# Attention with a threshold: each tile's bias from VectorE's product of scores and -c2

## The chip, the cores and the metric

The kernel runs on one core of a Trainium2 chip. The metric is the device time of one execution in microseconds. The kernel before takes 2197.92 us, the median of three runs (2195.69 to 2199.4).

## What is computed

Three blocks follow one another. The first is attention over 4 batches, 8 heads, 576 tokens and a head size of 64, in which each row keeps only the scores within tau (0.02) of its largest; then a gated MLP (512 to 1536 and back) behind an RMS norm; then a mixture of eight experts with weights P from eight Sinkhorn rounds. The part that the change touches:

```python
scores = scale * np.matmul(q, k.transpose(0, 1, 3, 2))
thresh = np.max(scores, axis=-1, keepdims=True) - tau
scores = np.where(scores >= thresh, scores, -1000000000.0)
scores = scores - np.max(scores, axis=-1, keepdims=True)
attn = np.exp(scores)
attn = attn / (np.sum(attn, axis=-1, keepdims=True) + 1e-09)
return np.matmul(attn, v).astype(np.float32)
```

## The kernel before, in words

All matrix products run in fp16 pairs (a high part and a remainder), so inputs are scaled by powers of two: `s_q` and `s_k` are the scales of q and k, `i_q` and `i_k` their inverses, and the score in PSUM is the true one times both scales.

Attention works in tiles of 128 query rows against all 576 keys: 32 tiles per batch of one head each (four chunks `c` of 128 tokens, eight heads) and four tiles of two heads for the remaining 64 tokens, so 36 per batch and 144 in all. `att_tile` does one of them:

- TensorE writes the scores S into PSUM, 128 x 576 in two banks (L282), from q and from the remainder of q. There are two score buffers.
- VectorE takes the maximum of each row, `mx` (L292).
- ScalarE multiplies `mx` by `wt`, which is -c2 (L293): the bias. Then it writes e = exp(c2 * S + bias) as fp32 to SBUF (L296), and adds `bt`, the scaled -tau, to `mx`: the threshold (L297).
- VectorE multiplies e by (S >= threshold) and sums the row in the accumulator (L298). After that the score buffer is free.
- ScalarE casts e to fp16 (L303), GpSimd subtracts for the remainder (L304 and L305), SP's queue transposes both by DMA into eT (L307). e, hl and eT have three buffers each.

`att_values` multiplies eT by v (L330), three tiles later (LAG is 3), issued behind the scores of a later tile. When a chunk's eight heads are through, `end_main` and `finish_x` normalise its rows and transpose them to xnT (L376 to L357). Two chunks make a token tile of the MLP: `mlp_in` (gv, L530, with the gating at L538 to L545) and `mlp_out` (x, L561). The weights of the MLP are prepared meanwhile by `prep_in` and `prep_out` (L432 to L509), and k, v and q of the next batch by `prepare` (L225, L256 and others). The expert block (h, L860; y, L906) comes after it.

The order on each engine is not written out: a planner sorts the instructions of every engine once, by priority, by its own simulated time and by when buffers come free. Attention has the higher priority, MLP work fills in. Once planned, each engine runs its list in order and stops at a wait.

`prep_q_scales` makes the factors of a batch, one column per chunk: `bt` (L207), `c2` (L209) and `wt` (L210), each in a buffer of its own batch. `mx`, the bias and the threshold are three columns of one small tile `nt` with four buffers.

Of the kernel before, what the change touches and what calls it, by code (L numbers as in the profile page):

```python
# [7 lines left out]
F32 = mybir.dt.float32  # L8
# [3 lines left out]
AF = mybir.ActivationFunctionType  # L12
ALU = mybir.AluOpType
AX = mybir.AxisListType
# [5 lines left out]
def kernel(  # L20
# [24 lines left out]
    V, A, G, T = nc.vector, nc.scalar, nc.gpsimd, nc.tensor  # L45
    B, H, S, D = q.shape
# [3 lines left out]
    P = 128  # L50
# [6 lines left out]
    NW = NCH + 1  # L57
# [3 lines left out]
    def small(shape, name, dt=F32, bufs=1):  # L61
        return p0.tile(shape, dt, tag=name, name=name, bufs=bufs)
# [80 lines left out]
    pa = pa_cm.__enter__()  # L143
# [19 lines left out]
    def norm_scale(sq, n, bits, name):  # L163

        return pow2_scale(sq, n, bits, name, 2.0**-60, True)
# [27 lines left out]
    def prep_q_scales(st):  # L193

        b, qr = st["b"], st["raw_q"]
        s_k, i_k = st["k"]
        qm = small([P, NW], "qm", bufs=2)
        for c in range(NW):
            sq = pa.tile([P, H, 2, D], F16, tag="ks", name=f"qq{b}_{c}", bufs=2)
            A.activation(  # L200
                sq[:, :, 0, :].bitcast(BF16), qr[:, :, c, :], AF.Square, accum_out=qm[:, c : c + 1]
            )
        s_q, i_q = norm_scale(qm, NW, 9, f"q{b}")

        wt = small([P, NW], f"wt_{b}")
        bt = small([P, NW], f"bt_{b}")
        V.tensor_scalar(bt, s_q, s_k[:, 0:1], ntau8[:, 0:1], ALU.mult, ALU.mult)  # L207
        c2 = small([P, NW], f"c2_{b}")
        V.tensor_scalar(c2, i_q, i_k[:, 0:1], z8[:, 0:1], ALU.mult, ALU.mult)  # L209
        V.tensor_scalar(wt, i_q, i_k[:, 0:1], nz8[:, 0:1], ALU.mult, ALU.mult)  # L210
        st.update(wt=wt, bt=bt, c2=c2, s_q=s_q)

    def prep_k(st, a):

# [56 lines left out]
    def att_tile(st, c, heads, slot, group):  # L271

        kT = st["kT"]
        qT, qX = st["q", c]
        nm = f"{st['b']}_{c}_{heads[0]}"
        sums = group["sums"]
        sp = psa.tile([P, 2, 512], F32, tag="S", name=f"S{nm}", bufs=2)
        rows = P // len(heads)
        for qq, first in ((qT, True), (qX, False)):
            for i, h in enumerate(heads):  # L280
                for j in range(2):
                    last = T.matmul(  # L282
                        sp[i * rows : (i + 1) * rows, j, 0:HS],
                        lhsT=qq[:, h, 0:rows],
                        rhs=kT[h // H2][:, h % H2, j * HS : (j + 1) * HS],
                        start=first,
                        stop=not first,
                    )
        sv = sp[:, :, 0:HS]
        nt = pa.tile([P, 3], F32, tag="nt", name=f"nt{nm}", bufs=4)  # L290
        mx = nt[:, 2:3]
        V.tensor_reduce(mx, sv, AX.XY, ALU.max)  # L292
        A.activation(nt[:, 0:1], mx, AF.Copy, scale=st["wt"][:, c : c + 1])  # L293
        e = pa.tile([P, S], F32, tag="e", name=f"e{nm}", bufs=3)
        ev = e.rearrange("p (a n) -> p a n", a=2)
        A.activation(ev, sv, AF.Exp, bias=nt[:, 0:1], scale=st["c2"][:, c : c + 1])  # L296
        A.activation(nt[:, 1:2], mx, AF.Identity, bias=st["bt"][:, c : c + 1])  # L297
        V.scalar_tensor_tensor(  # L298
            ev, sv, nt[:, 1:2], ev, ALU.is_ge, ALU.mult, accum_out=sums[:, slot : slot + 1]
        )  # L300

        hl = pa.tile([P, 2 * S], F16, tag="hl", name=f"hl{nm}", bufs=3)
        A.activation(hl[:, 0:S], e, AF.Copy)  # L303
        G.tensor_tensor(hl[:, S + REM :], e[:, 0 : NCH * P], hl[:, 0 : NCH * P], ALU.subtract)  # L304
        G.tensor_tensor(hl[:, S : S + REM], e[:, NCH * P :], hl[:, NCH * P : S], ALU.subtract)  # L305
        eT = pa.tile([P, 2 * S // P, P], F16, tag="eT", name=f"eT{nm}", bufs=3)
        nc.sync.dma_start_transpose(out=eT, in_=hl)  # L307
        waiting.append((st, heads, slot, group, eT))
        if len(waiting) > LAG:

            with tc.issue_after(last.ins):
                att_values(*waiting.pop(0))

    def att_values(st, heads, slot, group, eT):
        if slot == 0:
            group["pv"] = psa.tile([P, H * D], F32, tag="pv", name=f"pv{group['n']}", bufs=1)
        rows = P // len(heads)
        for i, h in enumerate(heads):
            vs, hh = st["vs"][h // H2], h % H2
            o = group["pv"][i * rows : (i + 1) * rows, slot * D : (slot + 1) * D]  # L320
            cols = slice(i * rows, (i + 1) * rows)
            mm = []
            for cc in range(NCH):
                mm.append((eT[:, cc, cols], vs[:, 0, hh, cc, :]))
                mm.append((eT[:, cc, cols], vs[:, 1, hh, cc, :]))
                mm.append((eT[:, NW + cc, cols], vs[:, 0, hh, cc, :]))
            mm.append((eT[:, NCH, cols], vs[:, 0, hh, NCH, :]))
            mm.append((eT[:, NCH, cols], vs[:, 1, hh, NCH, :]))
            for n, (a, r) in enumerate(mm):
                T.matmul(o, lhsT=a, rhs=r, start=n == 0, stop=n == len(mm) - 1)  # L330
        if slot == group["last"]:
            ended.append(group)
# [296 lines left out]
    def prepare(b, o):  # L629

        st = states[b]
        if o < NCH * H and o % H == 1:
            prep_q(st, o // H + 1)
        if b > 0 and o in (LAG - 3, LAG - 1):
            prep_v(st, (o - LAG + 3) // 2)
        if b + 1 == B:
            return
        nx = states[b + 1]
        early = b > 0
        if o == (4 if early else 20):  # L640
            nx["raw_k"] = load_raw("k", k, b + 1)
            nx["raw_v"] = load_raw("v", v, b + 1)
        if o == (10 if early else 23):
            prep_k_scale(nx)
        if o == (12 if early else 24):
            prep_v_scale(nx)
        if o == (18 if early else 26):
            prep_k(nx, 0)
        if o == 25:
            nx["raw_q"] = load_raw("q", q, b + 1)  # L650
        if o == 28:
            prep_q_scales(nx)
        if o == 32:
            prep_q(nx, 0)
        if o == 34:
            prep_k(nx, 1)

    st = states[0]
    for nm, src in (("k", k), ("v", v), ("q", q)):
        st["raw_" + nm] = load_raw(nm, src, 0)  # L660
    prep_k_scale(st)
    prep_q_scales(st)
    prep_q(st, 0)
    prep_k(st, 0)
# [6 lines left out]
    for t in range(len(row) + LAG):  # L671
        before = tc.cur_priority
        with attention_order():
            if t < len(row):
                b, c, heads, n, g = row[t]
                if n == 0:
                    g["sums"] = pa.tile([P, H], F32, tag="sums", name=f"sums{g['n']}", bufs=2)
                att_tile(states[b], c, heads, n, g)
                prepare(b, t % SLOTS)
            else:  # L680
                att_values(*waiting.pop(0))
            done = list(ended)
            ended.clear()
            for g in done:
                (end_main if g["c"] < NCH else end_rem)(g)
        first += tc.cur_priority - before
        for g in done:
            i = g["i"]
            if i == 1:
                for gi in range(NG):  # L690
                    prep_group(gi)
                first = tc.cur_priority
                tT = mlp_in(0)
                prep_out()
                mlp_out(0, tT)
            elif i is not None and i % 2 == 1 and i < len(tiles) - 1:
                mlp_out(i // 2, mlp_in(i // 2))
# [283 lines left out]
```

## Time and profile before

| what | value |
|---|---|
| median of three runs | 2197.92 us |
| profiled execution | 2195.02 us, its span 2193.2 us |
| TensorE (PE) busy | 2032.0 us, 93% |
| VectorE (DVE) busy | 1490.2 us, 68% |
| ScalarE (ACT) busy | 870.9 us, 40% |
| GpSimd (POOL) busy | 471.0 us, 21% |
| mean granted clock of TensorE | 0.98 |
| first and last scores (L282) | 38.9 and 610.6 us |
| first matmul of the MLP (gv, L530) | 156.7 us |

In the rows below times are in microseconds, and ns where that is said. A group's row has the line, the engine, the operation, what it writes and reads by the program's names, shapes, count, then busy time with the mean in ns of one, and idle time of the engine ahead of it. A row of waits has what waited, for whom, the total, how often and the longest. A row of the timeline has its start, its length, the engine and the instruction.

### The profile page before, as it was taken

How to read it: one execution, taken by the hardware profiler on the slowest of the kernel's cores; microseconds unless marked ns; L12 is line 12 of the kernel's file. 1: busy time of each engine (PE TensorE's matmuls, PEld its weight loads, DVE VectorE, ACT ScalarE, POOL GpSimd, SP SyncE). 2: the span in 40 equal slices, each digit the busy share in tenths (PEclk: the TensorE clock that was granted, in tenths of full speed). 3: DMA queues.
4: the chain of work that ended last, by engine and by line, in shares of the span. 5: the costliest groups of instructions: out<-in, count | busy, mean ns of one | idle time of the engine just before them, and what ended most of it. 6: DMA issues, size and time to landing. Idle time of an engine off the chain costs nothing.

```text
span 2193.2 us, 35334 instructions
## 1 busy us (share of the span) xinstructions
PE 2032.0 (93%) x13872; PEld 1194.7 (54%) x13872; DVE 1490.2 (68%) x3026; ACT 870.9 (40%) x1774; POOL 471.0 (21%) x572
## 2 busy tenths in 40 slices
PE   1358789899999999999999999999999999999999
PEld 0236667666876755545555555555555555555554
DVE  6999677777744287865775765766757757666554
ACT  6878778877843243311221221222212212222111
POOL 1347556665743231000000000000000000000000
PEclk9859999999999999999999999999999999999999
DMA  9895879867826051000100100100001001000001
GB/s 267 207 201 100 169 145 174 159 144 115 147 55 142 18 144 40 29 30 1 39 20 20 39 20 20 39 20 20 20 20 39 20 20 39 20 20 1 1 28 60
DMA packets 321879, 154.10 MB, mean 70 GB/s; under 512 B 278960, under 2 KB 292400, under 8 KB 321712
## 3 DMA queue, kind: packets, MB, share of 16 engines
q1 hardware_dynamic: 321120, 151.82, 30.4%
q8 instruction: 108, 1.77, 0.3%
q14 instruction: 59, 0.48, 0.1%
q0 software_dynamic: 64, 0.00, 0.0%
q10 hardware_dynamic: 528, 0.02, 0.0%
HBM read 68.18 MB, written 12.98 MB: 37 GB/s over the span
## 4 chain that ended last, share of the span: by engine, by line
PE 70%; DVE 2%; DMA 1%; SPq 1%; POOL 0%; issue 0%; ACT 0%; DVEq 0%; ACTq 0%
PE y L906 33%; PE h L860 28%; PE gv L530 5%; PE x L561 2%; PE pv L330 1%; DMA w1r<-in_moe_w_dram 1%; SPq L762 0%; PE S L282 0%; DMA x2T<-x2d 0%; DVE w L714 0%; DMA w2r<-in_moe_w_dram 0%; DMA eT<-hl 0%; PE logits L804 0%; DVE w1m L725 0%; POOL xh L601 0%
## 5 line engine op out<-in xcount | busy, mean ns | idle before, releaser
L860 PE MATMUL h<-x2T,w 128*128 128x384 f16 x4032 | 703.8, 326 | 9.9 <-DMA x2T<-x2d 3.9
L860 PEld LDWEIGHTS <-w 128*128 128x128 f16 x4032 | 394.1, 98 | 300.0 <-issue 14.2
L921 DVE SCALAR_TENSOR_TENSOR acc<-y,coef,acc 128x512 f32<-128x512 f32 x270 | 198.1, 746 | 283.0 <-PE y L906 282.9
L730 POOL TENSOR_TENSOR w1s<-w1r 128x512 f32<-128x512 f32 x16 | 20.3, 1271 | 1060.3 <-DMA w1r<-in_moe_w_dram 1006.3
L304 POOL TENSOR_TENSOR hl<-e,hl 128x512 f16<-128x512 f32 x144 | 172.8, 1200 | 228.2 <-ACT hl L303 146.2
L906 PE MATMUL y<-w,hD 128*128 128x512 f16 x864 | 219.9, 379 | 0.0
L906 PE MATMUL y<-w,hA 128*128 128x512 f16 x864 | 210.6, 379 | 0.9 <-DVE acc L921 0.6
L906 PE MATMUL y<-w,hC 128*128 128x512 f16 x864 | 210.0, 379 | 0.2 <-ACT acc L917 0.2
L906 PE MATMUL y<-w,hB 128*128 128x512 f16 x864 | 210.0, 379 | 0.0
L848 ACT ACTIVATE hA<-u 128x384 f16<-128x384 f32 x96 | 50.2, 522 | 341.1 <-DVE u L876 320.9
L848 ACT ACTIVATE hB<-u 128x384 f16<-128x384 f32 x96 | 50.2, 523 | 312.1 <-DVE u L880 311.2
L530 PE MATMUL gv<-xnT,wg 128*128 128x256 f16 x1296 | 167.8, 278 | 4.5 <-DVE u L540 3.0
L530 PE MATMUL gv<-xnT,wv 128*128 128x256 f16 x1296 | 167.5, 275 | 0.0
L330 PE MATMUL pv<-vs,eT 128*128 128x64 f16 (+1 forms) x2240 | 103.1, 201 | 50.3 <-DMA eT<-hl 47.3
L561 PE MATMUL x<-wo,tT 128*128 128x512 f16 x648 | 144.4, 379 | 1.0 <-DVE u L540 0.9
L906 PEld LDWEIGHTS <-hB 128*128 128x128 f16 x864 | 84.5, 98 | 101.9
L530 PEld LDWEIGHTS <-wg 128*128 128x128 f16 x1296 | 126.5, 100 | 24.0 <-issue 4.1
L298 DVE SCALAR_TENSOR_TENSOR e<-S,nt,e 128x576 f32<-128x576 f32 x144 | 116.3, 809 | 32.0 <-ACT e L296 31.5
L906 PEld LDWEIGHTS <-hD 128*128 128x128 f16 x864 | 84.6, 98 | 95.4
L530 PEld LDWEIGHTS <-wv 128*128 128x128 f16 x1296 | 126.4, 99 | 16.0 <-issue 0.2
L906 PEld LDWEIGHTS <-hC 128*128 128x128 f16 x864 | 84.7, 98 | 91.9 <-issue 0.3
L330 PEld LDWEIGHTS <-eT 128*128 128x128 f16 (+1 forms) x2240 | 91.0, 106 | 79.1 <-DMA eT<-hl 62.1
(244 smaller groups left out, 2852.1 us busy)
## 6 DMA issues: line engine op xcount, KB each, us to landing
w1r<-in_moe_w_dram SPq DMA_DIRECT2D x16, 1024.0 KB, 4.9
w2r<-in_moe_w_dram SPq DMA_DIRECT2D x16, 1024.0 KB, 5.3
wgatew<-in_moe_w_gate_dram SPq DMA_DIRECT2D x12, 512.0 KB, 6.0
wo<-in_moe_w_out_dram SPq DMA_DIRECT2D x12, 512.0 KB, 4.2
wvalw<-in_moe_w_val_dram SPq DMA_DIRECT2D x12, 512.0 KB, 4.5
x2d<-xs SPq DMA_DIRECT2D x24, 256.0 KB, 2.5
qX<-qT SPq DMA_DIRECT2D x40, 128.0 KB, 3.5
raw_k<-in_k_dram SPq DMA_DIRECT2D x4, 1024.0 KB, 6.2
```

The lines of the kernel that those rows point to most:

```text
L298: V.scalar_tensor_tensor(ev, sv, nt[:, 1:2], ev, ALU.is_ge, ALU.mult, accum_out=sums[:, slot : slot + 1])
L304: G.tensor_tensor(hl[:, S + REM :], e[:, 0 : NCH * P], hl[:, 0 : NCH * P], ALU.subtract)
L330: T.matmul(o, lhsT=a, rhs=r, start=n == 0, stop=n == len(mm) - 1)
L530: T.matmul(gv[:, a, :], lhsT=w[:, l, kk, f * P : (f + 1) * P], rhs=xt[:, r * KD + kk, :], start=n == 0, stop=n == 3 * KD - 1,)
L561: T.matmul(ps, lhsT=tT[f][:, l, o : o + P], rhs=wo[:, f, r, :], start=n == 0, stop=n == 3 * KF - 1,)
L730: G.tensor_tensor(sm[:, 0], a21, a22, ALU.add)
L848: A.activation(t[:, 0, :], src, AF.Relu)
L860: T.matmul(ps, lhsT=w[:, a, l, kk, f * P : (f + 1) * P], rhs=xb[:, b * 4 + r * 2 + kk, :], start=n == 0, stop=n == 5,)
L906: T.matmul(ps, lhsT=hs[a][f][:, l, jj * P : (jj + 1) * P], rhs=w2[:, r, f, :], start=n == 0, stop=n == 3 * KH - 1,)
L921: V.scalar_tensor_tensor(acc[i], ps, coef[h][:, i : i + 1], acc[i], ALU.mult, ALU.add)
```

## The change

The maximum over the scores is replaced by a product of the scores and `wt` that VectorE writes into e (where the exponential later overwrites it) and whose smallest value in each row goes through the accumulator into the first column of `nt`: since `wt` is negative, that is the bias itself. ScalarE's small multiplication falls away. The threshold is computed from the bias: times `w1`, which is 1 / (-(i_q * i_k) / 8), plus `bt`. `w1` is made per batch by two small VectorE operations. `wt`, `bt`, `c2` and `w1` share two buffers over the batches.

```diff
-        wt = small([P, NW], f"wt_{b}")
-        bt = small([P, NW], f"bt_{b}")
+        wt = small([P, NW], "wt", bufs=2)
+        bt = small([P, NW], "bt", bufs=2)
         V.tensor_scalar(bt, s_q, s_k[:, 0:1], ntau8[:, 0:1], ALU.mult, ALU.mult)
-        c2 = small([P, NW], f"c2_{b}")
+        c2 = small([P, NW], "c2", bufs=2)
         V.tensor_scalar(c2, i_q, i_k[:, 0:1], z8[:, 0:1], ALU.mult, ALU.mult)
         V.tensor_scalar(wt, i_q, i_k[:, 0:1], nz8[:, 0:1], ALU.mult, ALU.mult)
-        st.update(wt=wt, bt=bt, c2=c2, s_q=s_q)
+
+        w1 = small([P, NW], "w1", bufs=2)
+        V.tensor_scalar(w1, i_q, i_k[:, 0:1], -(float(D) ** -0.5), ALU.mult, ALU.mult)
+        V.reciprocal(w1, w1)
+        st.update(w1=w1, wt=wt, bt=bt, c2=c2, s_q=s_q)
...
-        nt = pa.tile([P, 3], F32, tag="nt", name=f"nt{nm}", bufs=4)
-        mx = nt[:, 2:3]
-        V.tensor_reduce(mx, sv, AX.XY, ALU.max)
-        A.activation(nt[:, 0:1], mx, AF.Copy, scale=st["wt"][:, c : c + 1])
+        nt = pa.tile([P, 2], F32, tag="nt", name=f"nt{nm}", bufs=4)
         e = pa.tile([P, S], F32, tag="e", name=f"e{nm}", bufs=3)
         ev = e.rearrange("p (a n) -> p a n", a=2)
+        V.tensor_scalar(
+            ev, sv, st["wt"][:, c : c + 1], None, ALU.mult, ALU.min, accum_out=nt[:, 0:1]
+        )
         A.activation(ev, sv, AF.Exp, bias=nt[:, 0:1], scale=st["c2"][:, c : c + 1])
-        A.activation(nt[:, 1:2], mx, AF.Identity, bias=st["bt"][:, c : c + 1])
+        A.activation(
+            nt[:, 1:2], nt[:, 0:1], AF.Identity, bias=st["bt"][:, c : c + 1],
+            scale=st["w1"][:, c : c + 1],
+        )
```

## Rows read from the trace of the kernel before

**Rows 1.** The page's chain that ended last: share of the span by engine.
```profile
PE 70%; DVE 2%; DMA 1%; SPq 1%; POOL 0%; issue 0%; ACT 0%; DVEq 0%; ACTq 0%
```

**Rows 2.** Busy time by stage: stretch, length, engines (instructions), granted clock, DMA share, GB/s.
```profile
41.00:157.00 116.00, 47.73 (x372) 27.05 (x371) 111.07 (x235) 97.15 (x201) 41.85 (x44) 0.75 0.85 206
157.00:300.00 143.00, 123.12 (x1340) 95.02 (x1339) 114.66 (x271) 112.14 (x263) 89.03 (x112) 0.97 0.73 143
300.00:612.00 312.00, 291.51 (x3222) 219.34 (x3219) 233.09 (x550) 245.04 (x567) 197.46 (x273) 0.98 0.79 145
```

**Rows 3.** Waits of TensorE from 40 to 160 us: total, times, longest.
```profile
PE pv L330 <- DMA eT<-hl: 24.6, 8, 4.7
PE S L282 <- DVE e L298: 19.1, 7, 6.9
```

**Rows 4.** The same from 160 to 620 us.
```profile
PE pv L330 <- DMA eT<-hl: 22.7, 21, 3.8
PE S L282 <- DVE e L298: 5.2, 5, 1.9
```

**Rows 5.** The tile nt: durations in ns, smallest, median, largest.
```profile
L292 DVE TENSOR_REDUCE nt<-S x144: 698/750/759, 41.4 to 611.2; 128x1 f32<-128x576 f32 x144
L293 ACT ACTIVATE nt<-nt,wt x144: 277/286/298, 44.3 to 612.0; 128x1 f32<-128x1 f32 x144
L297 ACT ACTIVATE nt<-nt,bt x144: 277/279/298, 44.5 to 612.2; 128x1 f32<-128x1 f32 x144
L298 DVE SCALAR_TENSOR_TENSOR e<-S,nt,e x144: 758/810/820, 48.4 to 613.2; 128x576 f32<-128x576 f32 x144
```

**Rows 6.** Timeline of VectorE from 130 to 142 us.
```profile
130.71 0.74 DVE L292 TENSOR_REDUCE nt<-S 128x1 f32<-128x576 f32 x1
131.37 0.47 DVE L336 TENSOR_SCALAR rsum<-sums 128x8 f32<-128x8 f32 x1
...
137.50 0.81 DVE L298 SCALAR_TENSOR_TENSOR e<-S,nt,e 128x576 f32<-128x576 f32 x1
138.24 0.08 DVE L298 DVE_READ_ACCUMULATOR e<-S,nt,e 128x1 f32 x1
138.24 0.68 DVE L436 SCALAR_TENSOR_TENSOR wo<-wo,wol 128x512 int32<-128x512 int32 x1
...
140.18 0.75 DVE L292 TENSOR_REDUCE nt<-S 128x1 f32<-128x576 f32 x1
```

**Rows 7.** Timeline of ScalarE from 128 to 148 us (start, length).
```profile
133.65 0.28 ACT L293 ACTIVATE nt<-nt,wt 128x1 f32<-128x1 f32 x1
...
134.95 0.81 ACT L296 ACTIVATE e<-S,nt,c 128x576 f32<-128x576 f32 x1
...
140.97 0.30 ACT L293 ACTIVATE nt<-nt,wt 128x1 f32<-128x1 f32 x1
...
141.35 0.82 ACT L296 ACTIVATE e<-S,nt,c 128x576 f32<-128x576 f32 x1
```

**Rows 8.** Timeline of TensorE: the first matmuls of the MLP.
```profile
156.66 2.74 PE L530 MATMUL gv<-xnT,wg 128*128 128x256 f16 x12 [1.36 <-DMA xnT<-xn]
```

**Rows 9.** Groups by line, shapes apart, of VectorE and of ScalarE.
```profile
L920 DVE TENSOR_SCALAR acc<-acc,coef 128x512 f32<-128x512 f32 x18 | 7.3, 478 | 0.0
L210 DVE TENSOR_SCALAR wt<-q_i,k_i,nz 128x5 f32<-128x5 f32 x4 | 1.2, 300 | 0.0
...
L200 ACT ACTIVATE qq<-raw_q 128x512 bf16<-128x512 f32 x20 | 12.4, 621 | 6.2 <-DMA raw_q<-in_q_dram 6.1
L346 ACT ACTIVATE xn<-x,v_i 128x512 bf16<-128x512 f32 x16 | 11.4, 712 | 3.8 <-DMA xnT<-xn 3.8
```

**Rows 10.** Timeline of VectorE and GpSimd at two of three places.
```profile
248.39 0.75 DVE L292 TENSOR_REDUCE nt<-S 128x1 f32<-128x576 f32 x1
249.11 0.31 POOL L305 TENSOR_TENSOR hl<-e,hl 128x64 f16<-128x64 f32 x1
...
403.59 1.48 DVE L292 TENSOR_REDUCE nt<-S 128x1 f32<-128x576 f32 x2
404.65 0.30 POOL L305 TENSOR_TENSOR hl<-e,hl 128x64 f16<-128x64 f32 x1
```

## The prediction

> **What bounds the kernel now.** I first followed the chain that ended last: TensorE alone is 70% of the span [rows 1], and the chain reaches back only into the end of the attention stage. So the end is TensorE's total work plus the time in which it stood idle or ran at its lower clock. The change takes no matmul away; it can only fill idle time ahead of 612 us, where the last attention tile ends.
>
> Busy time by stage [rows 2] sizes that. From the first attention tile to the first matmul of the MLP (41 to 157 us) TensorE is busy 47.7 of 116 us, at a granted clock of 0.75 (so half of that stretch at 1.2 GHz), while VectorE is busy 111.1 of 116. From 157 to 300 us TensorE lacks 19.9 us, from 300 to 612 us 20.5 us. All three together, 68.3 + 19.9 + 20.5 = 108.7 us, cap any gain but for the clock.
>
> Then the waits of TensorE in these stages. Before 160 us it waits 24.6 us in 8 places for the transposed probabilities eT and 19.1 us in 7 places for VectorE's last pass over the scores, which frees the score buffer [rows 3]. From 160 to 620 us the same two waits are 22.7 us in 21 places and 5.2 us in 5 [rows 4]. Both hang on one chain per tile: scores, maximum (VectorE), bias copy (ScalarE), exponential (ScalarE), masked product (VectorE), cast, subtraction, transposing DMA. The first MLP matmul at 156.66 waits for xnT, which is made from the first sixteen tiles [rows 8]: the speed of this chain decides when TensorE gets filler work at all.
>
> **The change part by part.**
>
> *The bias copy goes.* It takes 0.286 us, 144 times [rows 5]. Copy, threshold and exponential start at 140.97, (next) and 141.35, so a small ScalarE instruction holds the queue 0.19 us [rows 7]: 144 x 0.19 = 27 us of ScalarE's time.
>
> *The threshold gets a scale read from a tile* beside its bias. The trace has a pair that differs by such a scale alone: 712 ns for the square of x with one (L346) and 621 for that of q without (L200) [rows 9], so 0.09 us per tile, 13 us in all. ScalarE keeps 27 - 13 = 14 us. It is busy 245 of 312 us from 300 to 612 us, 79% [rows 2], so this shortens queues and is no term by itself.
>
> *The maximum becomes a product that is written and a minimum read from the accumulator.* The reduction takes 0.750 us [rows 5], and the next instruction starts 0.66 us after it [rows 6]. No row has VectorE multiply a wide tile out of PSUM by a scalar. From below: such a product inside SBUF, 128x512, takes 478 ns [rows 9]; from above: the masked product of the same scores, with a scalar per row, a written tile and an accumulator, takes 0.810 us, its accumulator read starts 0.74 us after it and the next instruction at the same 0.74 [rows 5, 6]. I take the upper end, for that row reads the same scores in the same way: 0.81 us, 0.08 us later in the queue, and the minimum is there 0.82 us after the start in place of 0.75. That is 144 x 0.08 = 12 us more of VectorE; the lower end, about 0.51 us for 576 columns by its length, would give VectorE back 144 x 0.24 = 35 us.
>
> The Trainium skill ("VectorE: DVE Perf Modes", section "Why PSUM operands drop a tier") says that an operand in PSUM leaves one read port, so that fp32 runs at one element per clock; the sum by it is the one that I make. The tier table above it on that page allows a scalar operation up to twice that from any PSUM, which is the lower end and one of the rivals.
>
> *The chain gets shorter.* At 140.18 a reduction starts; it ends at 140.93, the copy starts at 140.97, the exponential at 141.35, 1.17 us after the reduction began [rows 6, 7]. With the change: 0.82 us for product and read, 0.04 us to ScalarE, 0.86 us in all: 0.31 us less. This is the tight case. Where ScalarE puts other work between copy and exponential it is more: the reduction of 130.71 has its copy at 133.65 and its exponential at 134.95 [rows 6, 7], and one turn in ScalarE's queue instead of two would save up to 1.2 us. I take 0.31, because a stall of the list that I can't see will take the place of the rest.
>
> - Up to 157 us: eighteen tiles, in nine pairs (two score buffers), come before the matmuls of the second token tile can be closed. 9 x 0.31 = 2.8 us earlier filler. VectorE has only 116 - 111.1 = 4.9 us free there, so without pushing weight work back no more than 4.9 could be had.
> - From 157 to 612 us: 26 waits of TensorE, 27.9 us, each 0.31 shorter: 8.1 us at most. Some are shorter than 0.31 and some end by something else; I take 7.
>
> *What it costs.* In the full stretch up to 157 us each 0.08 us of VectorE counts: 23 tiles, 1.8 us. The weight preparation behind it in the queue (L435, L466) comes later by that, and so does all that TensorE gets from it. The two new small operations for w1 run once per batch; the nearest row is the 0.30 us of wt (L210) [rows 9], so 0.6 us before the first scores, and hidden for the other three batches by idle VectorE. The new buffers of wt, bt and c2 (two, where each batch had its own) make batch 2 wait for batch 0, long done: nothing.
>
> *A new wait.* The product writes e, so VectorE, not ScalarE, now waits until GpSimd has read the e of three tiles before, and about 1.1 us earlier in the tile. Laying the starts of the reductions against the ends of GpSimd's second subtraction, VectorE would come too early in 3 of 141 tiles: at 248.39 against 249.11 + 0.31, and lastly with the second of the pair from 403.59, which starts at 404.31, against 404.65 + 0.30 [rows 10]. These two and the third between them are some 2.2 us of VectorE, with stalls of the MLP's gating (L539, L540) behind them; at 75% load [rows 2] about 0.8 us of it reaches TensorE. Nothing is moved past a DMA queue: no transfer is added, the transposes of eT on SP only get their data earlier.
>
> Sum: -2.8 - 7 + 1.8 + 0.6 + 0.8 = -6.6 us. The profiled execution took 2195.0 us (span 2193.2), 2.9 below the median of 2197.9; on the median the sum gives 2191.3, called **2191**.
>
> **The rivals.**
>
> *Nothing measurable.* VectorE is full up to 157 us, so a shorter chain there only trades places with weight work, which L561 needs later; and after 157 us a wait for eT may end by the DMA itself. For it: the waits are 1.1 us in the mean, of a chain that takes several us. Against it: 26 of them lie on one chain. Then the terms -7 and -2.8 shrink to about what the costs are: 2198, within 4.4 us (0.2%, what a measurement of this kernel can tell from no change).
>
> *Slower by the buffer of e.* The product holds e from the start of the tile, and three buffers are passed on by GpSimd, which is in no hurry: it waits and then works in bursts. If its end comes later than the product in the second tile of most pairs, VectorE stops with everything behind it. It decides when the slack, 3 failing tiles now, turns negative in about half of the 72 pairs: 36 x 0.6 us (the shortest of the two stalls shown) = 22 us of VectorE, of which the full stage passes on all and the later ones about half, 13 us; with 3 us left of the chain's gain 2198 + 13 - 3 = 2208. For it: the second tile of a pair comes right behind the first (two reductions in 1.48 us [rows 10]). Against it: the order of the queues is planned anew with this wait known.
>
> *Slower by the planned order.* The planner sorts all queues by its own costs; a changed tile moves every lull. One more such as the wait of 4.9 us for L571, and the clock falling with it, is 8 us: 2206. It needs no shorter or longer instruction, and nothing in the profile speaks against it.
>
> *The product runs at two elements per clock.* Then VectorE has 0.24 us per tile back instead of 0.08 lost: 23 x 0.32 = 7 us more in the full stretch, 2184. Against it: every wide read of PSUM in this trace takes about one element per clock [rows 5].
>
> **How the numbers follow.** The forecast has 0.38; twice the rate 0.05; nothing measurable 0.29; the buffer of e 0.18; the planned order 0.10. Faster by over 0.2% (under 2193.5) is 0.38 + 0.05 = 0.43, within 0.2% 0.29, slower 0.28. The likeliest case by itself reaches from 2182 (1.2 us instead of 0.31 in the nine pairs is 8 us more, the waits at 8.1 another) to 2193. The range takes in the slow rivals at 2206 and 2208 and the fast one: 2177 to 2210.
>
> **What would show it.** In the new profile the product should take about 0.81 us with an accumulator read of 0.08; ScalarE should have 144 fewer small instructions and thresholds of 0.37 us; the exponential should start 0.04 us behind the accumulator read in tight tiles; the first gv matmul should come 2 to 5 us before 156.7; TensorE's waits for eT and for the masked product should fall by about 10 us together ahead of 612 us. Wrong would be: VectorE idle in front of the product because of GpSimd (the buffer of e), TensorE's idle time unchanged with a shorter chain (nothing measurable), or new lulls at places where this chain isn't (the order).

## The result, and the profile after

The kernel after takes 2218.88 us (median; 2218.36 to 2221.45), the kernel before 2198.66 us beside it: a ratio of 1.0098 [1.0083, 1.0113], some 20 us slower. The forecast was 2191 with a range up to 2210, so it was wrong in sign, and the time lies outside the range. Two causes carry nearly all of it, and neither is the duration of an instruction that was changed: the queues were planned into a worse order (about 10 us with the new instructions), and the small tiles that the change shares moved all buffers that lie behind them by 128 bytes (about 8 us).

Busy time by stage of the kernel after, in the columns of [rows 2]:

```profile
41.00:157.00 116.00, 49.30 (x379) 28.40 (x380) 113.57 (x252) 93.90 (x174) 41.32 (x43) 0.79 0.82 195
157.00:300.00 143.00, 117.88 (x1273) 90.37 (x1272) 118.48 (x308) 110.37 (x230) 85.70 (x110) 0.95 0.74 146
300.00:612.00 312.00, 282.52 (x3096) 212.79 (x3094) 235.60 (x617) 232.59 (x466) 191.32 (x261) 0.97 0.78 144
```

Up to 157 us TensorE does a little more than before (49.3 us against 47.7). From 157 to 612 us it does 14.2 us less (123.12 + 291.51 before, 117.88 + 282.52 now), in 193 fewer matmuls; these have to be made up at the end, where nothing but TensorE counts. ScalarE got relief (9.6 us less over the whole span, 870.9 us before and 861.3 after, where 14 were forecast), VectorE its extra work (20.2 us more, 1490.2 and 1510.4, where 12 were forecast).

The waits of TensorE after, from 40 to 160 us and then from 160 to 620 us (total, times, longest), which answer to [rows 3, 4]:

```profile
PE pv L337 <- DMA eT<-hl: 18.0, 7, 4.3
PE S L286 <- DVE e L305: 15.5, 10, 4.4
```

```profile
PE pv L337 <- DMA eT<-hl: 33.1, 34, 2.8
PE S L286 <- DVE e L305: 11.2, 6, 5.3
```

Early the two waits fell by 10 us together; later they rose by 16 us, and the wait for eT has 34 places instead of 21. That is the term of the forecast that went the wrong way.

The instructions themselves, by line and tile (smallest, median and largest ns), against [rows 5]:

```profile
L297 DVE TENSOR_SCALAR_CACHE_REDUCE e<-S,wt x144: 759/812/822, 44.4 to 622.3; 128x576 f32<-128x576 f32 x144
L301 ACT ACTIVATE nt<-nt,bt,w x144: 370/376/397, 48.4 to 624.8; 128x1 f32<-128x1 f32 x144
```

The product takes 0.81 us, the threshold 0.376 us. A tight tile on VectorE, with the accumulator read of 0.08 us, and its exponential and threshold on ScalarE (start, length):

```profile
142.32 0.81 DVE L297 TENSOR_SCALAR_CACHE_REDUCE e<-S,wt 128x576 f32<-128x576 f32 x1
143.06 0.08 DVE L297 DVE_READ_ACCUMULATOR e<-S,wt 128x1 f32 x1
```

```profile
143.23 0.83 ACT L300 ACTIVATE e<-S,nt,c 128x576 f32<-128x576 f32 x1
143.96 0.38 ACT L301 ACTIVATE nt<-nt,bt,w 128x1 f32<-128x1 f32 x1
```

From the start of the product to the exponential are 0.91 us; from the start of the reduction it was 1.17 us before [rows 6, 7]. Over all 144 tiles the smallest is 0.84 us (1.13 before) and the median 1.11 us (1.78 before).

That takes the order of ScalarE's queue as well. Here the threshold stands behind the exponential, in all 144 tiles. In the kernel before it stands ahead of it, in all 144 tiles, as in the tile of [rows 7] between 140.97 and 141.35:

```profile
141.16 0.28 ACT L297 ACTIVATE nt<-nt,bt 128x1 f32<-128x1 f32 x1
```

So the chain did get shorter, and the kernel slower all the same. That made the question: where are the 20 us?

### The profile page after: what moved, and what is told of

Read it like the earlier page. It is cut to its first block, busy times and chain, and to the rows that moved or that the text cites. A ratio compares the mean times of both kernels' runs of the same rounds, so it can differ in the third digit from the quotient of the medians.

```text
span 2219.6 us, 35389 instructions
## 1 busy us (share of the span) xinstructions
PE 2042.4 (92%) x13872; PEld 1198.7 (54%) x13872; DVE 1510.4 (68%) x3178; ACT 861.3 (39%) x1630; POOL 470.2 (21%) x572
## 4 chain that ended last, share of the span: by engine, by line
PE 73%; DMA 7%; DVE 7%; issue 3%; ACT 2%; POOL 2%; SPq 1%; ACTq 0%; DVEq 0%; POOLq 0%
PE y L913 33%; PE h L867 28%; PE gv L537 7%; DMA eT<-hl 4%; PE x L568 3%; DVE e L297 1%; PE S L286 1%; DMA qT<-qs 1%; PE pv L337 1%; DMA wo<-in_moe_w_out_dram 1%; DVE e L305 1%; ACT e L300 1%; DMA w1r<-in_moe_w_dram 1%; POOL hl L311 1%; SPq L769 1%
## 5 line engine op out<-in xcount | busy, mean ns | idle before, releaser
L297 DVE TENSOR_SCALAR_CACHE_REDUCE e<-S,wt 128x576 f32<-128x576 f32 x144 | 115.7, 810 | 34.9 <-PE S L286 29.9
```

The lines of the kernel that those rows point to most:

```text
L297: V.tensor_scalar(ev, sv, st["wt"][:, c : c + 1], None, ALU.mult, ALU.min, accum_out=nt[:, 0:1])
```

## The experiments

All ratios are to the kernel before, run beside on the same chip; 0.001 is 2.2 us. "On its own order" means that the queues were planned for that kernel; "on before's order" that the order of every queue was written out.

### First: the edits one at a time, each with a plan of its own

The theories were *plan* (the new order of the queues costs the time), *buffer* (e is held from the head of the tile) and *VectorE* (0.08 us more in a full queue).

**w1only**: the kernel before, with only the shared small tiles and the operations for w1, which nobody reads.

```diff
-        wt = small([P, NW], f"wt_{b}")
-        bt = small([P, NW], f"bt_{b}")
+        wt = small([P, NW], "wt", bufs=2)
+        bt = small([P, NW], "bt", bufs=2)
...
-        c2 = small([P, NW], f"c2_{b}")
+        c2 = small([P, NW], "c2", bufs=2)
...
+        w1 = small([P, NW], "w1", bufs=2)
+        V.tensor_scalar(w1, i_q, i_k[:, 0:1], -(float(D) ** -0.5), ALU.mult, ALU.mult)
+        V.reciprocal(w1, w1)
```

Expected:

> The kernel before with only the small tiles changed: wt, bt and c2 in two shared buffers and the two operations for w1 per batch, which nothing reads. Theory 'plan' (the new order of the queues costs the 20 us, not the tile's instructions): eight tiny operations already re-sort the lists, so the time moves by more than 4.4 us, either way, without any lasting work added. Theory 'buffer' (e is held from the head of the tile) and theory 'VectorE' (0.08 us more per tile in a full queue): 2198, within 4.

Measured: 2210.89 us, 1.0059 [1.0041, 1.0076]. Eight operations that feed nothing (223 and 178 ns) and three shared tiles cost 13 us. I took this for the plan's doing; most of that reading fell later.

**thr**: w1only, and the threshold made from the bias; maximum and copy stay.

```diff
-        A.activation(nt[:, 1:2], mx, AF.Identity, bias=st["bt"][:, c : c + 1])
+        A.activation(
+            nt[:, 1:2], nt[:, 0:1], AF.Identity, bias=st["bt"][:, c : c + 1],
+            scale=st["w1"][:, c : c + 1],
+        )
```

Expected:

> As w1only, and the threshold is made from the bias by w1 with two operands from tiles; maximum and bias copy stay. It adds 0.09 us of ScalarE to each tile. Theory 'plan': again another order, a time that has no relation to w1only's, 2185 to 2225. Theories 'buffer' and 'VectorE': 2198 to 2202, for ScalarE isn't the bound.

Measured: 2215.43 us, 1.0091 [1.0068, 1.0114].

**mxe**: before, with the maximum written into the first column of e, so that e is held as long as in the kernel after.

```diff
-        mx = nt[:, 2:3]
+        mx = e[:, 0:1]
```

The exponential writes over that column, so it stands behind the threshold here.

Expected:

> The kernel before, but the maximum is written into the first column of e, so that e is held from the reduction on as in the changed kernel; no instruction is added. Theory 'buffer': most of the 20 us, 2210 to 2220. Theory 'VectorE': 2198, within 4. Theory 'plan': anywhere from 2185 to 2225, no nearer to the changed kernel than the others.

Measured: 2201.48 us, 1.0021 [1.0008, 1.0033], with an order of its own that differs from before's from the 279th step of TensorE on. So holding e longer cost 4.5 us here (1.8 to 7.3 us), its new order included, and not most of the 20 us.

**inplace**: after, but the product goes back over the scores, so e is free until the exponential; the threshold lies tau from the bias, and w1, bt and c2 are gone.

```diff
-            ev, sv, st["wt"][:, c : c + 1], None, ALU.mult, ALU.min, accum_out=nt[:, 0:1]
+            sv, sv, st["wt"][:, c : c + 1], None, ALU.mult, ALU.min, accum_out=nt[:, 0:1]
...
+        A.activation(ev, sv, AF.Exp, bias=nt[:, 0:1], scale=-1.0)
+        A.activation(nt[:, 1:2], nt[:, 0:1], AF.Identity, bias=tau8[:, 0:1])
...
-            ev, sv, nt[:, 1:2], ev, ALU.is_ge, ALU.mult, accum_out=sums[:, slot : slot + 1]
+            ev, sv, nt[:, 1:2], ev, ALU.is_le, ALU.mult, accum_out=sums[:, slot : slot + 1]
```

Expected:

> The changed kernel, but the product is written back into the score buffer, not into e: e is held from the exponential on as before. Exponential with scale -1, threshold is bias plus tau, mask by is_le, no w1, c2 and bt. VectorE's product is as long as in the change (0.81 us). Theory 'buffer': 2190 to 2200. Theory 'VectorE': 2212 to 2222, as the change. Theory 'plan': a third order, 2185 to 2225.

Measured: 2223.85 us, 1.0122 [1.0105, 1.0139]: slower still with e free and w1 gone. As the cause of the 20 us, the buffer falls here.

### Second: the order of every queue written out

At the end of the kernel's function each engine's instructions are chained in a written order, by edges that only fix the order of issue and add no wait:

```python
    dep = mybir.DependencyInfo(mybir.DependencyClass.NoSync, mybir.DependencyReason.DATA)
    for engine, order in written_orders.items():
        for a, b in zip(order, order[1:]):
            tc.add_manual_dep(ins[engine][b], ins[engine][a].name, dep, reason="order")
```

**w1only_bo**: w1only on before's order (only these lines are added). Expected:

> The kernel before with the eight unread VectorE operations for w1 and the shared small tiles (the edit that alone took 2210.9 us), but with the planned order of every queue written out as it was in the kernel before: each engine's instructions are chained in that order, and the two new operations of a batch stand right behind the one that makes wt. Theory plan (the 13 to 20 us come from the new order of the queues, not from any instruction): the time falls back to that of before, 2196 to 2199 us, ratio 0.999 to 1.001. Theory VectorE (more work in a full VectorE queue is what costs): the eight operations are still there, so some 2205 to 2211 us, ratio 1.004 or more. Theory buffer has no part in this kernel: as before, 2197 us.

Measured: 2206.13 us, 1.0045 [1.0031, 1.0059]. That is in the range of the theory VectorE (2205 to 2211), not in the plan's: the order explains 3 us of the 13, no more than the uncertainty of the two ratios. What holds the other 10 is shown only below.

**after_bo**: the kernel after on before's order. Expected:

> All instructions of the kernel after, with the order of every queue written out as in the kernel before: the product with its minimum stands where the maximum stood, the copy on ScalarE is missing from its place, the two operations for w1 stand behind the one for wt. Theory plan: no slower than before, and now the forecast's own sum can be seen: 2190 to 2198 us, ratio 0.997 to 1.000; the waits of TensorE for eT between 160 and 620 us come back from 33 us to 23 us or less. Theory VectorE (the product's 0.08 us more in each tile, in a queue that is full, costs the time): still 2210 us or more, ratio 1.006 or more. Theory buffer (e is taken from the head of the tile): 2201 to 2206 us.

Measured: 2208.04 us, 1.0050 [1.0036, 1.0063]. Half of the loss is gone, half stays; no theory gave this.

**before_ao**: the kernel before on the order of after. Expected:

> All instructions of the kernel before, with the order of every queue written out as in the kernel after: the maximum stands where the product stood, the copy on ScalarE right ahead of its Exp, the operations for w1 are missing. Theory plan: as slow as the kernel after or slower, 2214 to 2224 us, ratio 1.008 to 1.012, with the waits of TensorE for eT between 160 and 620 us at 30 us or more. Theories VectorE and buffer (the cost lies in the new instructions): the old instructions bring the time back to 2196 to 2201 us.

Measured: 2216.81 us (2209.24 to 2222.7), 1.0085 [1.0067, 1.0102]. The old instructions, at their old places in memory, are as slow as the new kernel, and TensorE's waits from 160 to 620 us are nearly those of the kernel after:

```profile
PE pv L330 <- DMA eT<-hl: 32.8, 33, 5.3
```

For the masked product TensorE waits 10.4 us in 9 places (11.2 in 6 in the kernel after). So the waits in 33 or 34 places belong to the order, whichever instructions run in it. With the instructions of before this order costs 19 us (15 to 22).

What was left of w1only_bo had to come from something that no queue shows. Laid beside the kernel before, matmul by matmul in the same order, it was late from the first loads on (1.9 us at 20 us).

### Third: the place of the buffers

Sharing the tiles gives back 128 bytes per partition, so everything behind the small tiles lies 128 bytes lower: the buffers raw, into which q, k and v are loaded, begin at 22144 instead of 22272 = 87 x 256. The buffers right behind raw (ks, qT, qX, kT and vs) lie as far past a multiple of 256 as raw does, in every kernel here, and later the expert block's loads go to the same addresses; "the place of raw" below means all of these. The first load of q (columns: KB, median us from issue to landing), in before and in before_sh2:

```profile
raw_q<-in_q_dram SPq DMA_DIRECT2D x1, 1024.0 KB, 8.3
```

```profile
raw_q<-in_q_dram SPq DMA_DIRECT2D x1, 1024.0 KB, 10.1
```

In after it takes 10.0 us, in after_pad 8.4. Over all runs: with raw at a multiple of 256 bytes 7.9 to 8.5 us in nine kernels and 9.2 in one (thr_bo_pad); elsewhere 9.6 to 10.1 us in seven. It is the start of the kernel, where transfers take 0.98 of the time; the later loads of the same buffers, between other work, show no such split (6.2 us before, 5.8 in before_sh2 for the second q). The transposes from ks into qT do: in the median of 20 they land after 2.9 or 3.0 us in the ten kernels with raw at a multiple of 256, and after 3.3 to 3.8 us in the other seven.

**before_sh2**: before with wt and bt shared; same instructions, same order of every queue, only 128 bytes lower.

```diff
-        wt = small([P, NW], f"wt_{b}")
-        bt = small([P, NW], f"bt_{b}")
+        wt = small([P, NW], "wt", bufs=2)
+        bt = small([P, NW], "bt", bufs=2)
```

Expected:

> The kernel before, with wt and bt of the four batches in two shared buffers each instead of four. Instructions and the order of every queue are those of before; the small tiles end 128 bytes earlier, so that raw, kT, qT, qX, vs, e, hl and eT all lie 128 bytes lower in each partition (raw at 22144, which is no multiple of 256, instead of 22272 = 87 x 256). Theory place (some of the loss is where the buffers lie: the first load of raw_q took 8.2 to 8.5 us in the three kernels with raw at 22272, 9.6 to 10.1 us in the six with another place): 2203 to 2209 us, ratio 1.003 to 1.006, with that load at 9.6 us or more. Theory plan alone: nothing changes, 2196 to 2199 us. Theory VectorE or any other that puts the loss on the new instructions: 2196 to 2199 us too.

Measured: 2203.10 us, 1.0024 [1.0014, 1.0034], 5 us. The first score matmul (start, length) in before, then in before_sh2:

```profile
38.94 0.64 PE L282 MATMUL S<-kT,qT 128*128 128x288 f16 x2 [1.02 <-DMA kT<-ks]
```

```profile
41.64 0.64 PE L282 MATMUL S<-kT,qT 128*128 128x288 f16 x2 [0.83 <-DMA kT<-ks]
```

ScalarE's first work on the loaded q (L200) starts at 16.72 us in before and at 18.40 here, so 1.7 of these 2.7 us follow that load. At 680 us the lag is 5 us, at the end of these two executions 7.7 us; past the first tiles it can't be told from scatter, for before_right, which takes as long as before, is 3 us late at the end of its profiled execution.

**after_pad**: after with an unused small tile of 128 bytes, which brings raw back to 22272; same order as after.

```diff
+    small([P, 32], "pad")
     dram = ctx.enter_context(tc.tile_pool(name="dram", bufs=1, space=DRAM))
```

Expected:

> The kernel after with an unused small tile of 128 bytes, which brings every large buffer back to its place of before (raw at 22272); instructions and order of the queues are those of after. Theory place: the first load of raw_q is back at 8.2 to 8.5 us, and the time falls by the 9 us that this place costs, to 2207 to 2213 us, ratio 1.005 to 1.007; what is left is the plan's. Theory plan alone: still 2215 to 2222 us. Theory VectorE: still 2215 to 2222 us.

Measured: 2210.57 us, 1.0062 [1.0047, 1.0077]: 128 unused bytes make the kernel after 8 us faster.

**after_bo_pad**: both, before's order and the pad. Expected:

> All instructions of the kernel after, in the order of before and with the large buffers at their places of before. If plan and place together are the whole loss, the forecast's own sum is left over: 2191 to 2200 us, ratio 0.997 to 1.001. Theory VectorE (the product's 0.08 us in a full queue is dear): 2203 us or more, ratio 1.003 or more. With place without effect it stays at 2206 to 2209 us.

Measured: 2201.81 us, 1.0015 [1.0006, 1.0025]. The four kernels with the instructions of after make a square:

| instructions of after | raw at 22144 | raw at 22272 |
|---|---|---|
| order planned for after | 1.0098 | 1.0062 |
| order of before | 1.0050 | 1.0015 |

The order is worth 0.0048 in one column and 0.0047 in the other, the place 0.0036 and 0.0035 in the rows (each with about 0.002 of uncertainty): within that they add up. Order and instructions do not: with the instructions of before, at the same place, the order costs 0.0085 (before_ao), 0.0038 more than the 0.0047 here, with an uncertainty of 0.0025. Of the page's first lines these are the busy times of after, then span and busy times of after_pad and of after_bo_pad:

```profile
PE 2042.4 (92%) x13872; PEld 1198.7 (54%) x13872; DVE 1510.4 (68%) x3178; ACT 861.3 (39%) x1630; POOL 470.2 (21%) x572
```

```profile
span 2210.4 us, 35389 instructions
PE 2041.5 (92%) x13872; PEld 1199.6 (54%) x13872; DVE 1506.5 (68%) x3178; ACT 861.6 (39%) x1630; POOL 472.8 (21%) x572
```

```profile
span 2200.4 us, 35438 instructions
PE 2031.7 (92%) x13872; PEld 1194.3 (54%) x13872; DVE 1501.1 (68%) x3178; ACT 860.8 (39%) x1630; POOL 470.0 (21%) x572
```

The place comes as idle time of TensorE: from after to after_pad the span falls by 9.2 us (from 2219.6), busy time by 0.9. The order comes in this pair as busy time: the same 13872 matmuls take 9.8 us less in the old order, idle time (168.9 and 168.7 us) is the same. In other pairs it is both: from after to after_bo busy time falls by 10.1 us and idle time by 5.1; from before to before_ao they rise by 14.1 and 13.6. From 157 to 612 us the granted clock is 0.96 in after_pad and 0.98 in after_bo_pad; 0.02 of 455 us is 9 us, so TensorE's lower level (1.2 GHz) around the waits would be enough for it. But before_sh2, on the order of before, has 0.96 there too: that the clock is the way in which the order costs its time is not shown.

**before_hl**: before's order and places, except that e, hl and eT begin at a multiple of 256 bytes, where they were 192 bytes past one (wt, bt and c2 shared as in w1only, and two tiles moved in front of raw):

```diff
-        nt = pa.tile([P, 3], F32, tag="nt", name=f"nt{nm}", bufs=4)
+        nt = p0.tile([P, 3], F32, tag="nt", name=f"nt{nm}", bufs=4)
...
-                    g["sums"] = pa.tile([P, H], F32, tag="sums", name=f"sums{g['n']}", bufs=2)
+                    g["sums"] = p0.tile([P, H], F32, tag="sums", name=f"sums{g['n']}", bufs=2)
```

Expected:

> The kernel before in its own order, with raw, kT, qT, qX and vs at their places of before, but e, hl and eT moved from 192 bytes past a multiple of 256 to a multiple of 256 (wt, bt and c2 share two buffers each, nt and the sums lie in front of raw instead of in front of e). Theory place in its wide form (every transfer that starts off a multiple of 256 bytes is longer): the 144 transposes of hl into eT get shorter than their 3.4 us, TensorE's waits for eT fall, and the time to 2185 to 2194 us. In its narrow form (only the loads into raw and the weights' loads suffer): 2196 to 2199 us, as before.

Measured: 2200.44 us, 1.0014 [1.0005, 1.0023]. The transposes did get faster: in the median of 144 they land after 2.9 us here, and after 3.4 us in each of the sixteen other kernels, where hl and eT are off the multiple. TensorE's waits for eT from 160 to 620 us fell too, from 22.7 us [rows 4]:

```profile
eT<-hl SPq DMA_TRANSPOSE x144, 2.9
```

```profile
PE pv L330 <- DMA eT<-hl: 17.2, 19, 3.2
```

The kernel gained nothing by it. Other waits grew (S for the masked product 8.1 us, 5.2 before; one of 3.9 us for ScalarE's bias, L293, that before doesn't have). So half a microsecond less in the chain of the median tile, with the order held, brought no gain. What makes this kernel 3 us slower than before, the moved small tiles or something else, is not shown.

**before_right**: the weights' buffers, 224 bytes past a multiple of 256 so far, moved onto one by an unused tile at the end of their pool, with wt, bt and the scales of v shared to make room:

```diff
+    pw.tile([P, 56], F32, tag="pad", name="pad")
     pw_cm.__exit__(None, None, None)
```

Expected:

> The kernel before in its own order, all buffers on the left moved down by 256 bytes (raw stays at a multiple of 256, e and hl stay 192 bytes past one), and the buffers of the weights and of the gated units, which began 224 bytes past a multiple of 256, moved down by 224 bytes onto one. If the rule of place holds for the loads of the weights too: their loads (512 KB, 6.4 us median before) land sooner, the start of the kernel, where transfers are busy 98% of the time, gets shorter, and the time falls to 2185 to 2195 us. If only raw's place counts: 2196 to 2199 us.

Measured: 2198.36 us, 0.9999 [0.9989, 1.0009]; the loads of w_gate in the first 45 us took 6.3 us (6.4 before). Of the places, only that of raw and the buffers that share its offset has shown an effect on the time; which of them carries it is not separated. The order is written out in this kernel too, so the edges by themselves cost nothing that can be measured.

### Fourth: what is left on the old order and place

**w1only_bo_pad**, the eight operations alone. Expected:

> Before's order, before's places of the large buffers, and of the change only the shared small tiles and the eight unread operations for w1 (about 0.06 us each, 0.5 us in all). If the product with its minimum carries the 4 us that after_bo_pad lost: 2196 to 2200 us, ratio 0.999 to 1.001. If operations that are added to VectorE's full queue carry them: 2201 to 2203 us, ratio 1.0015 or more.

Measured: 2202.18 us, 1.0012 [1.0002, 1.0022]. By its trace the operations take 0.35 and 0.19 us, not 0.06.

**thr_bo_pad**, with the scaled threshold. Expected:

> As w1only_bo_pad, and the threshold made from the bias by w1 (0.37 us instead of 0.28 us on ScalarE, 144 times, behind the copy instead of beside it); the maximum and its copy stay. If the product carries the loss: 2196 to 2200 us. If the threshold does (the masked product waits for it): 2201 us or more, and after_bo_pad's 2201.8 us is then its price less the gain of the copy.

Measured: 2205.28 us (2198.91 to 2210.51), 1.0028 [1.0013, 1.0043]. With after_bo_pad at 1.0015 the steps are +0.0012, +0.0016 and -0.0013, each about as large as its uncertainty; it seems that the operations for w1 and the longer threshold cost, and the missing copy gives back, but the three runs don't settle it.

**inplace_bo_pad**: inplace, whose own order and place gave 2223.85 us, on those of before. Expected:

> The kernel inplace (product written back over the scores, no w1, no bt, no c2, no copy of the maximum; 2223.9 us on its own order and places) with the order of every queue of before and raw back at 22272. If order and place carried its whole loss: 2199 us or less. If the shorter chain from the scores to Exp is worth what the forecast said (-6.6 us): 2189 to 2195 us. If an order planned for the old instructions can't use a shorter chain: 2197 to 2202 us.

Measured: 2195.41 us, 0.9994 [0.9985, 1.0003]. Order and place were its whole loss, 28 us. The gain over before can't be told from zero: at most 3.3 us, where the forecast had 6.6. TensorE waits 20.5 us in 19 places for eT from 160 to 620 us, against 22.7 in 21 [rows 4]: each wait is as long as before.

This does not test a chain that is 0.31 us shorter, for on the order of before the chain hardly gets shorter. That order holds the threshold ahead of the exponential. A tight tile of after_bo_pad, product first:

```profile
143.31 0.81 DVE L298 TENSOR_SCALAR_CACHE_REDUCE e<-S,wt 128x576 f32<-128x576 f32 x1
```

```profile
144.17 0.39 ACT L302 ACTIVATE nt<-nt,bt,w 128x1 f32<-128x1 f32 x1
144.46 0.81 ACT L301 ACTIVATE e<-S,nt,c 128x576 f32<-128x576 f32 x1
```

From product to exponential are 1.15 us, against 1.17 before. Over all 144 tiles the median is 1.62 us in after_bo_pad and 1.66 in inplace_bo_pad, against 1.78 before; on the order of after it is 1.07 in after_pad and, with the old instructions, 1.66 in before_ao. So the chain gets much shorter only by both together, the copy gone and the threshold behind the exponential.

On the same order and place inplace_bo_pad is 0.0021 below after_bo_pad (1.0015), and their intervals don't overlap. VectorE waits 4.8 us in 8 places for GpSimd's hl in after_bo_pad and nowhere in inplace_bo_pad, so holding e may be part of this; the operations for w1, bt and c2 and the scale of the threshold differ too. No version beats the kernel before by a margin that was measured.

## Why the prediction was wrong

*Right.* The durations: product 0.81 us (0.81 forecast), read 0.08, threshold 0.376 (0.37), 144 fewer copies. The Trainium skill ("VectorE: DVE Perf Modes", section "Why PSUM operands drop a tier") has fp32 from PSUM at one element per clock, and the 0.81 us agree with it; the tier table's upper rate does not show. The chain in a tight tile of the new plan: 0.26 us shorter in the tile shown, 0.29 between the smallest of each kernel (0.31 forecast). The buffer of e: VectorE waits 2.3 us in 4 places for GpSimd's hl (2.2 us in 3 places forecast), and the rival built on it, as the cause of a large loss, fell with inplace.

*Wrong: the 26 waits of TensorE, each 0.31 us shorter, the term of -7.* It took the waits of one plan as fixed places and shortened each of them. On the new order TensorE waits 44.3 us in 40 places for the two (27.9 in 26 before): 16 us more instead of 7 less.

The old order doesn't give the term either: after_bo_pad waits 23.4 us in 24 places for eT, inplace_bo_pad 20.5 in 19. There the 0.31 us itself is missing. It was worked out from a tile in which copy, threshold and exponential follow one another [rows 7], as if the exponential came next behind the product; the threshold between them was left out, and where the order keeps it there the chain of a tight tile is 1.15 us, not 0.86. before_hl is the nearer test of a shorter chain on a held order, by 0.5 us in the transposes, and it gained nothing. That is the rival "nothing measurable"; why a wait that gets shorter in one place grows in another is not shown.

*Not shown: the term of -2.8.* The first gv matmul was to come 2 to 5 us earlier than 156.7. It came at 156.1 us, at 154.4 in after_pad, and on the order of before later (159.0 in after_bo_pad, 158.6 in inplace_bo_pad). In before_right and before_hl, with the instructions and the order of before, it came at 157.8 and 158.5, so 1 to 2 us are scatter. Nor are the costs (+1.8, +0.6, +0.8) measured one by one: on the old order and place the whole change stands at 3 us more (1.0015), where the sum had 6.6 less.

*Wrong: the planned order at 0.10.* The mechanism was named, and its size (8 us) was near the 10 us measured. It got a low chance because the profile of before can show nothing of an order that isn't made yet. That should have raised it: the planner sorts some 19,000 instructions anew after any change to the tile, here with other operations, durations and buffers. The order of before came out better than that of after with either set of instructions: on after's order the instructions of before take 1.0085 [1.0067, 1.0102].

*Wrong: "The new buffers of wt, bt and c2 ... nothing".* I asked only what they would wait for. They also moved raw and all that lies behind it by 128 bytes, and that was 8 us, a term that neither forecast nor rivals had. The Trainium skill ("DMA: Bandwidth & Descriptors", section "How a descriptor splits into AXI transactions") says that a read which does not start at a multiple of 256 B begins at the one below and fetches bytes that it doesn't use. Here the read side did not move, only the place in SBUF that is written, so the page doesn't state this case; that loads of rows of 1 KB got longer by 1.6 us fits its boundary. So do the transposes of hl in before_hl, where the side that is read moved too (2.9 us on the multiple, 3.4 off it). The weights' loads showed nothing, which sets a limit to it.

*Also wrong, on the way:* my reading of w1only as the plan's work. Of its 13 us, 3 are the order's (1.0059 to 1.0045, within the uncertainty) and 7 the place's (1.0045 to 1.0012). And 478 ns for 512 columns are by length 0.54 us for 576, not 0.51; that moves only the price of the rival with two elements per clock, by less than 1 us.

*Open.* Which exchange of instructions makes after's order the worse one; how the place of raw and its neighbours comes to cost more than the 1.7 us of the first load; and whether the new instructions are worth something on the new order: after_pad (1.0062 [1.0047, 1.0077]) against before_ao (1.0085 [1.0067, 1.0102]), same order and same place, and a chain whose median is 1.07 against 1.66 us, would be 5 us in their favour, but the intervals overlap.

## What to carry to other kernels

Where a planner orders the queues, a change of a few instructions is two changes: chain the instructions in the old order and run it once, and the order's share stands by itself, for that set of instructions (10 us with the new ones here, 19 with the old). Then look whether the old order lets the change act at all: here it kept the threshold ahead of the exponential. Look at the addresses too: a tile of 20 bytes that is added or dropped moves everything behind it, and a kernel that starts on its transfers may pay for that. A wait seen in one plan is not yet a place where time can be saved by a shorter chain; even with the plan held, faster transposes gained nothing (before_hl).

## What the runs showed of the hardware

- The first 1 MB load of q, in rows of 1 KB, lands in 7.9 to 8.5 us where its buffer begins at a multiple of 256 bytes (9.2 once), and in 9.6 to 10.1 us where it begins 128 or 192 bytes past one. With all buffers from raw to eT moved by 128 bytes, same instructions and same order, the kernel takes 1.0024 [1.0014, 1.0034] of its time.
- DMA transposes of 128 x 1152 fp16 from hl into eT land in 2.9 us where both begin at a multiple of 256 bytes (before_hl), and in 3.4 us in all sixteen kernels where they begin 64, 128 or 192 bytes past one; those from ks into qT in 2.9 to 3.0 us against 3.3 to 3.8. The kernel with the faster eT was not faster (1.0014 [1.0005, 1.0023]).
- Weight loads into buffers 224 bytes past such a multiple (before_right) gained nothing by being moved onto it (6.4 and 6.3 us).
- A product of PSUM scores with a minimum in the accumulator takes 0.81 us for 128x576 fp32, and the next instruction starts 0.74 us after it, as for the masked product.
